# The last six chunks as three wide blocks, the weight sums on POOL, and two plain chunks ordered by a modelled clock

## The chip, the core and the metric

The kernel runs on one core of a Trainium2 chip: TensorE (PE, with its weight loads as PEld), VectorE (DVE), ScalarE (ACT), GpSimd (POOL) and SyncE (SP), whose queue issues nearly all transfers. The metric is the device time of the program in microseconds (us), a median over executions of one program.

## The reference

Windowed attention for 8 batches, 8 heads, 576 positions and 64 values a head, half of the heads with a dilation of 4, and behind it two matrix products with an ELU between them:

```python
attn = exp(scores - max) / (sum + 1e-9)          # window of 32, dilation 1 or 4
x = (attn @ v)  as  4608 tokens x 512
h = x @ w_in                                      # 512 x 2048
g = where(h > 0, h, exp(min(h, 0)) - 1)
out = g @ w_out                                   # 2048 x 512
```

## The kernel before, in words

**Precision.** A float32 product runs as three products of a faster format: each operand is split into a rounded part (a cast) and what is left (the "rest", the operand less its rounded part), and high x high, high x low and low x high are summed in PSUM. A cast is ACT's as a rule, a rest is DVE's.

**Tokens.** The 4608 tokens are nine chunks of 512. Chunks 0, 1 and 2 are *plain*: for each of 16 blocks `f` of 128 hidden units, 12 products make `h` in a PSUM bank, the ELU and the split are done, and 12 products add the block to four output banks `o_ps`. In chunk 0 the first blocks run in full float32, and the weights arrive and are converted there.

**Chunks 3 and 4 are *combined*** (`combined_chunk`): the first matrix product is done by a scheme of seven products in place of eight (Winograd's form of Strassen's), with sums of weight blocks (S1 to S4) and of token blocks (T1 to T4, made by `moving_operand`). A step has 12 products of 256 columns. The second matrix product stays plain: 16 blocks, 4 token tiles and 3 products each, 192 of 512 columns a chunk, taken from a list `fifo` between the steps.

**Chunks 5 to 8 are two *wide blocks*** (`wide_chunk`) of two chunks each. Both matrix products use the scheme there, `inner` for the first (28 units of 12 products of 512 columns) and `outer` for the second (28 units of 12). `make_unit` makes a unit's operand ahead of time, `summed` the token sums that it needs.

**Weights.** The sums of the weights' blocks are made on the chip and written to DRAM (`combined`, `sums_out`). The sums of the first weights are made in `combine`, on DVE with casts on ACT, in chunks 1 and 2; those of the second in `combine_out`, on POOL with casts on ACT, in chunks 3 to 5. `load_combined` brings each unit's weights, 512 KB, back into a ring `r0` of four, on SP's queue.

**Attention.** Batches 0 and 1 are done in chunk 0. A *piece* is either the scores of a pair of heads (36 small products of 64 columns) or its outputs (12 of 96 columns), put between other products. For batches 2 and 3, `scores_piece` and `outputs_piece` do two pairs at a time, in three banks (both `a_ps` and `h1`), at blocks named by `WHEN`; from chunk 3 on `pieces` does one pair at a time, in the two `a_ps` banks. Later batches' outputs go by DRAM (`outputs`) until their token chunk comes.

**What sets the order.** In chunks 0 to 2 a scheduler orders the instructions, held by `issue_after` where the program says so. From chunk 3 on the program order holds: `clock` models the time of PE, DVE, ACT and POOL, `side` holds lists of steps (softmax, weight sums), and `work(until)` issues those steps that the modelled clock can finish by a time. Each engine, and each queue, takes its instructions in order.

In a plain chunk after the first, ACT copies `h` out of its PSUM bank (`elu`, L874), and exp (L879), a relu (L888) and the max step (L889) read the copy. Chunks 1 and 2 use one bank `h0` for this, since `h1` is a pieces' bank. L149 is `mm`, which issues every product; L629 is `Ordered`, which issues all that the modelled clock orders; in the changed program these are L146 and L606.

Of the kernel before, what the change touches and what calls it, by code (L numbers as in the profile page):

```python
# [24 lines left out]
P = 128  # L25
# [8 lines left out]
LASTC = NCH - 4  # L34
# [16 lines left out]
ORDER = "A11 S2 S3 A12 S1 A22 S4".split()  # L51
STORED = "A11 A12 S2 S4 S3 S1 A22".split()
MOVING = "B11 T2 T3 B21 T1 T4 B22".split()
POPS = (3, 4, 0, 4, 0, 5, 0)
FIRST_POPS = (2, 2, 1, 2, 1, 1, 2), (3, 4, 3, 2, 0, 4, 0)
TODO = [t.split() for t in ("u1 exp0< relu0< rest1<", "u2 elu0< cast0<", "u3 rest0<", "C11", "C22", "C21 exp1 relu1 push1", "elu1 C12 cast1 push0")]
OPERANDS = [t.split() for t in ("", "cast:B11 make:T1", "rest:B11", "make:T2 cast:T2", "rest:T2", "make:T3", "cast:T3 rest:T3",
                                "cast:B21 rest:B21", "make:T4 cast:T1", "rest:T1 cast:T4", "rest:T4 cast:B22", "rest:B22", "", "")]
WHEN = {1: (0, 6, 7, 13), 2: (1, 6, 7, 12)}
LAST = 14  # L60
OPER = 12
PLAIN = ("a5", "a-1'", "a3'", "a4'", "r1'", "r2'")
HALVED = {(2, 3): 4}
COMBINE = {(1, 11): 0, (1, 13): 1, (1, 15): 2, (2, 2): 3, (2, 4): 4, (2, 6): 5, (2, 9): 6, (2, 11): 7}
PLAN = {36: "R5", 52: "X0", 55: "X2"}
WIDE_PLAN = {5: "R6"}
OUTPUTS_FROM = 7
KEPT_UNTIL = 18
PIECES_AT = range(7, 42)
COMBINE_AT = {2: "F0", 4: "C0", 6: "W0", 8: "F1", 10: "C1", 12: "W1", 14: "F2", 16: "C2", 18: "W2", 36: "F3", 39: "C3", 40: "W3", 41: "F4", 44: "C4", 45: "W4", 46: "F5", 49: "C5", 50: "W5"}  # L70
WIDE_COMBINE = {9: "F6", 13: "C6", 14: "W6", 15: "F7", 18: "C7", 19: "W7"}
FIRST = 6
# [3 lines left out]
KEEP = {0: (14, 15, 12, 13, 0, 1, 2, 3), 3: (4, 5), 4: (6, 7), 6: (8, 9), 8: (10, 11)}  # L76
# [8 lines left out]
WIDE_OPERANDS = {(2, 3): "cast:B11", (2, 4): "rest:B11", (3, 1): "cast:B21", (3, 2): "rest:B21"}  # L85
WIDE_FIRST = {"A11": "make:T1 make:T2 cast:T2 rest:T2", "A12": "cast:T1 rest:T1 make:T3", "S2": "cast:T3 rest:T3 make:T4", "S1": "cast:T4 rest:T4", "S3": "cast:B22 rest:B22"}
STORE_LAG = 1
STEP = 1.28
# [3 lines left out]
LANDING = 6.0  # L92
TOLERANCE = 0.3
SURE = -3.0
ENDING = 1.9
EASE = 0.4
OVERRUN = (1.5, 2.5, 1.5, 2.5, 2.5, 2.5, 1.0)
# [6 lines left out]
def body(ctx: ExitStack, tc: tile.TileContext, q, k, v, masks, w_in, w_out, out, out_t):  # L104
# [24 lines left out]

    raw2, raw, full4, full2, full = [None] * (NF // 2), [None] * NF, [None] * (NF // 2), [None] * NF, [None] * 2 * NF  # L130
# [15 lines left out]
    def mm(to, w, x, **kw):  # L146
        n = length(x)
        clock["PE"] += n * (4.0 if x.dtype == F32 else 1.0) / 2400 if n != 2 * G else 0.062
        return inorder(nc.tensor.matmul(to, w, x, **kw))  # L149
# [1527 lines left out]
```

## Time and profile before

| | |
|---|---|
| median of 3 runs | 849.73 us (849.23 to 850.75) |
| the profiled execution's own time | 847.88 us |
| its span, first to last instruction | 846.1 us |
| mean granted TensorE clock | 0.998 |
| busy: PE, DVE, ACT, POOL | 830.7, 642.2, 546.5, 76.7 us |
| read from and written to HBM | 148.0 and 49.5 MB |

A group's row reads: line, engine, operation, output <- inputs, shapes, count | busy us, mean ns of one | idle us of the engine just before, and what ended it. A row of a stage reads: from:to, length, busy us (count) of PE, PEld, DVE, ACT and POOL, granted clock, share of the DMA engines, GB/s. A float32 product of 64 or 96 columns has two records, so 12 products of 96 columns show as x24. Chunk 1 begins near 127 us, chunk 3 near 318, the first wide block at 515, the last at 690.

### The profile page before, as it was taken

The numbers are of one execution on the slowest core, as the hardware profiler recorded it, in microseconds if no ns is written. First come the engines' busy times: TensorE is split into PE (matmuls) and PEld (weight loads), VectorE is DVE, ScalarE is ACT, GpSimd is POOL, SyncE is SP. The second block draws the span as 40 slices with busy tenths as digits, with TensorE's granted clock in tenths as the row PEclk, the third lists the DMA queues.
The fourth block names the chain that finished last, engine by engine and source line by source line (L and its number), as shares of the span: only waits on it lengthen the run. The fifth ranks groups of instructions, "written<-read, shape, count | busy, mean of one in ns | idle before, by whom it ended". The sixth has DMA issues, their size and how long they took to land.

```text
span 846.1 us, 16853 instructions
## 1 busy us (share of the span) xinstructions
PE 830.7 (98%) x6696; PEld 676.1 (80%) x6696; DVE 642.2 (76%) x871; ACT 546.5 (65%) x935; POOL 76.7 (9%) x78
## 2 busy tenths in 40 slices
PE   6999999999999999999999999999999999999998
PEld 5566888888888887888888988878788888888886
DVE  6999998868588878788676777584879763466992
ACT  5888776645655556677667767667964535686450
POOL 3000000000000002330011330013202020000000
PEclk9999999999999999999999999999999999999999
DMA  9997466532687877998889995667756677666665
GB/s 308 371 380 298 133 186 222 170 114 100 205 252 250 244 205 254 317 322 259 242 262 336 322 324 186 236 187 253 255 182 202 194 245 216 193 196 196 195 212 169
DMA packets 105934, 198.67 MB, mean 235 GB/s; under 512 B 13216, under 2 KB 58112, under 8 KB 105600
## 3 DMA queue, kind: packets, MB, share of 16 engines
q1 hardware_dynamic: 105712, 197.29, 71.9%
q8 instruction: 53, 0.87, 0.4%
q10 hardware_dynamic: 144, 0.31, 0.1%
q14 instruction: 25, 0.20, 0.1%
HBM read 148.02 MB, written 49.55 MB: 233 GB/s over the span
## 4 chain that ended last, share of the span: by engine, by line
PE 95%; DMA 2%; DVE 1%; ACT 1%; SPq 1%; issue 0%; POOL 0%; DVEq 0%; ACTq 0%; POOLq 0%
PE o_ps L149 48%; PE h L149 35%; PE a_ps L149 11%; DMA outputs<-gl 1%; DMA r<-combined 1%; DMA qt<-q 0%; PE a L149 0%; ACT pt L538 0%; PE b L149 0%; SPq L319 0%; DVE nmx L498 0%; POOL r L463 0%; DVE pt L536 0%; PE d L149 0%; DVE sm L463 0%
## 5 line engine op out<-in xcount | busy, mean ns | idle before, releaser
L149 PE MATMUL o_ps<-a,r 128*128 128x512 f32 x672 | 159.6, 390 | 0.0
L149 PEld LDWEIGHTS o_ps<-a,r 128*128 128x128 f32 x672 | 125.1, 188 | 25.8
L149 PE MATMUL h<-x,r 128*128 128x256 f32 (+1 forms) x708 | 131.2, 335 | 0.4 <-issue 0.4
L149 PEld LDWEIGHTS h<-x,r 128*128 128x128 f32 x708 | 108.5, 189 | 16.6 <-ACT x L629 0.8
L149 PE MATMUL o_ps<-r,r 128*128 128x512 f32 x384 | 93.6, 389 | 0.0
L149 PE MATMUL h<-a,r 128*128 128x512 f32 (+1 forms) x456 | 89.3, 347 | 1.4 <-ACT e L629 1.3
L149 PEld LDWEIGHTS h<-a,r 128*128 128x128 f32 x456 | 73.5, 189 | 13.8 <-ACT e L629 1.8
L149 PEld LDWEIGHTS o_ps<-r,r 128*128 128x128 f32 x384 | 71.6, 188 | 14.6
L149 PE MATMUL o_ps<-a,gh 128*128 128x512 f32 x216 | 75.1, 445 | 0.0
L149 PEld LDWEIGHTS o_ps<-a,gh 128*128 128x128 f32 x216 | 40.2, 188 | 17.3 <-issue 10.5
L874 ACT COPY h<-h 128x512 f32<-128x512 f32 x30 | 17.5, 582 | 40.0 <-PE h L149 39.9
L149 PE MATMUL o_ps<-r,gh 128*128 128x512 f32 x128 | 40.2, 395 | 0.0
L149 PE MATMUL a_ps<-a,r 128*128 128x512 f32 x168 | 39.4, 389 | 0.0
L894 DVE TENSOR_TENSOR gl<-e,gh 128x512 fp32r<-128x512 f32 x37 | 25.4, 686 | 17.5 <-ACT gh L893 17.1
L149 PEld LDWEIGHTS a_ps<-a,r 128*128 128x128 f32 x168 | 31.5, 188 | 6.5
L629 ACT COPY pt<-sm 32x384 f32<-32x384 f32 x48 | 24.5, 510 | 17.2 <-DVE sm L629 16.5
L629 ACT ACTIVATE x<-x 128x1024 f32<-128x1024 f32 (+1 forms) x33 | 34.9, 1056 | 0.5
L149 PE MATMUL h<-x,a 128*128 128x512 f32 (+1 forms) x128 | 34.3, 416 | 0.0
L149 PEld LDWEIGHTS a_ps<-pt,vt 128*64 128x64 f32 x640 | 27.2, 137 | 8.4 <-issue 5.2
L629 POOL TENSOR_TENSOR h<-h 128x256 f32<-128x256 f32 x24 | 23.8, 993 | 109.6 <-DMA kt<-k 51.8
L149 PE MATMUL a_ps<-pt,vt 128*64 128x96 f32 x640 | 31.9, 250 | 0.1
L149 PE MATMUL o_ps<-a,gl 128*128 128x512 f32 x80 | 31.3, 391 | 0.0
(259 smaller groups left out, 1631.4 us busy)
## 6 DMA issues: line engine op xcount, KB each, us to landing
r<-combined SPq DMA_DIRECT2D x112, 512.0 KB, 4.6
r<-sums_out SPq DMA_DIRECT2D x32, 512.0 KB, 4.6
r<-plain_out SPq DMA_DIRECT2D x24, 512.0 KB, 4.3
vt<-v SPq DMA_DIRECT2D x30, 384.0 KB, 4.7
kt<-k SPq DMA_DIRECT2D x29, 304.0 KB, 4.4
qt<-q SPq DMA_DIRECT2D x30, 288.0 KB, 4.3
r<-w_in SPq DMA_DIRECT2D x16, 512.0 KB, 6.9
r<-w_out SPq DMA_DIRECT2D x16, 512.0 KB, 7.7
```

What stands on the lines that cost most here:

```text
L149: return inorder(nc.tensor.matmul(to, w, x, **kw))
L629: return inorder(getattr(self.eng, name)(**kw))
L874: copied.append(a.copy(out=h, in_=h_ps).ins)
L894: low.append(v.tensor_tensor(out=gl, in0=e, in1=gh.bitcast(F32), op=ALU.subtract).ins)
```

## The change

- Chunks 3 to 8 are three wide blocks. `combined_chunk`, its operands and its list of steps are gone; plain chunks remain for 0, 1 and 2.
- Chunks 1 and 2 (`plain_chunk`) are now in program order by the modelled clock too. A block's ELU and split are steps (`own_steps`) that go first; `late_steps` (splits of weights), softmax steps and weight sums follow as they fit. After each run of 12 products (`slot`) one piece, of one pair, may be put.
- exp and the max step read `h` in its PSUM bank; the copy is gone, and the banks `h0` and `h1` alternate.
- All 16 weight sums are jobs (`start_sums`) whose adds, casts and rests are on POOL, from block 7 of chunk 1 into the first wide block. Some softmax steps and splits of weights go to POOL or to their own engine, whichever the clock frees first (`better`). In the first wide block POOL makes the token sums of `summed`, and operands are made at most four units ahead.
- The outputs of batch 4 go by DRAM too, and the first weights of the wide blocks are loaded in block 14 of chunk 2.
- The modelled clock has new prices for products, for POOL and for what POOL adds to DVE.

Three places in the instruction lists show what moves. First TensorE, in the part that was the first combined chunk; `h_4246` and `h_4353` are its two banks, `o_ps` a bank of the second product. Before:

```order
L149 MATMUL h_4246<-r_1358,r_934 128x256 x12
L149 MATMUL h_4353<-x_3440,r_934 128x256 x12
L149 MATMUL o_ps<-a_1961,a_1626 128x512 x2
L149 MATMUL o_ps<-a_1961,a_1681 128x512
L149 MATMUL o_ps<-a_1961,a_1626 128x512 x2
L149 MATMUL o_ps<-a_1961,a_1681 128x512
```

Now, at the entry of the first wide block, with products of chunk 2 between its first units:

```order
L146 MATMUL a_ps_4072<-r_1352,r_932 128x512 x6
L146 MATMUL a_ps_4073<-r_1352,r_932 128x512 x6
L146 MATMUL o_ps<-r_1321,gh 128x512 x2
L146 MATMUL o_ps<-r_1321,gl 128x512
```

A unit's 12 products have 512 columns instead of 256, and there are half as many units for the same tokens.

Second, the sums of the first weights. Before, they stand on DVE in chunks 1 and 2, among the ELU's steps (`a_2284` holds a pair of weight blocks):

```order
L894 TENSOR_TENSOR gl<-e,gh 128x512
L302 TENSOR_TENSOR a_2284<-a_2284 128x256
L606 STREAM_TRANSPOSE pt_79<-sm 32x12x32 x6
L303 TENSOR_TENSOR a_2284<-a_2284 128x256
L889 SCALAR_TENSOR_TENSOR e<-h,e 128x512
L304 TENSOR_TENSOR a_2284<-a_2284 128x256
L305 TENSOR_TENSOR a_2284<-a_2284 128x256
L894 TENSOR_TENSOR gl<-e,gh 128x512
L309 TENSOR_TENSOR a_2284<-a_2284,e 128x512 x2
```

Now they stand on POOL, in the second half of chunk 1, with their casts and with softmax steps (`a_2073` holds the weights):

```order
L606 TENSOR_TENSOR sm<-sm,nmx 96x768
L606 TENSOR_TENSOR a_2073<-a_2073 128x256 x7
L606 COPY pt_79<-hh 32x12x32
L606 CAST e<-a_2073 128x512
L606 TENSOR_TENSOR a_2073<-a_2073 128x256
L606 CAST e<-a_2073 128x512
L606 TENSOR_TENSOR a_2073<-a_2073,e 128x512
L606 TENSOR_TENSOR sm<-sm,sums 96x768
L606 TENSOR_TENSOR a_2073<-a_2073,e 128x512
```

Adds, casts and rests of a sum follow each other on one engine, and DVE has none of them.

Third, the entry of the first wide block in the changed program. On DVE, from the last block's max step to the rest of T2 (`x_4088` is T1, `x_4089` T2, `a_1644` and `a_1745` T2's two parts, `a-1_3421` holds a softmax and the first columns of batch 4):

```order
L606 SCALAR_TENSOR_TENSOR e<-h_4022,e 128x512
L606 TENSOR_REDUCE sums<-a-1_3421 96x12
L606 TENSOR_TENSOR gl<-e,gh 128x512
L606 TENSOR_SCALAR sums<-sums 96x12
L606 RECIPROCAL sums<-sums 96x12
L606 TENSOR_TENSOR x_4088<-x_2761,x_1957 128x2x192
L606 TENSOR_TENSOR x_4088<-x_2761 128x2x64
L606 TENSOR_TENSOR x_4088<-a-1_3421,x_2761 128x2x256
L606 TENSOR_TENSOR x_4089<-x_2761,x_4088 128x2x192
L606 TENSOR_TENSOR x_4089<-x_2761,x_4088 128x2x64
L606 TENSOR_TENSOR x_4089<-a-1_3421,x_4088 128x2x256
L606 TENSOR_TENSOR a_1745<-x_4089,a_1644 128x2x512
```

And on SP's queue there (`r_932` is the ring of weights, `combined` the weight sums and blocks in DRAM):

```order
L315 DMA sums_out_113<-gh 128x2x256
L952 DMA r_932<-combined_89 128x1024
L315 DMA sums_out_113<-gh 128x2x256
L913 DMA out<-gh 128x512
L315 DMA sums_out_113<-a_2073 128x2x256
L913 DMA out<-gh 128x512
L913 DMA out<-gl 128x512
L952 DMA r_932<-combined_88 128x1024
L315 DMA sums_out_113<-a_2073 128x2x256
L952 DMA r_932<-combined_88 128x1024
L340 DMA x_4088<-whole_out_106 128x1024
```

Before, T1 to T4 were made in chunk 2, and stores of POOL's sums stood between weight loads in the combined chunks.

The diff, cut to its core:

```diff
-LASTC = NCH - 4
+LASTC = NCH - 6
...
+FILL = 4.2
+EARLY = 0.0
+HOME = {2: 1, 3: 2, 4: 2.4, 5: 3.2, 6: 3.2, 7: 4.2}
+LEAD = 4
+SLOWING = 0.1
...
-        clock["PE"] += n * (4.0 if x.dtype == F32 else 1.0) / 2400 if n != 2 * G else 0.062
+        clock["PE"] += PIECES.get(n) or n * (4.0 if x.dtype == F32 else 1.0) / 2400 + 0.0133
...
-    def combine(p):
...
-        nc.vector.tensor_tensor(out=a22, in0=a21, in1=a22, op=ALU.add)
...
-            nc.scalar.copy(out=h, in_=w)
-            nc.vector.tensor_tensor(out=l, in0=w, in1=h.bitcast(F32), op=ALU.subtract)
...
+    def start_sums():
+
+        for half in (0, 1) if phase[0] < 3.4 else (2,):
+            if not jobs or busy[half] == "running" or (busy[half] or 0.0) > clock["PE"]:
+                continue
+            start_sum(half)
+
+    def start_sum(half):
...
+        nc.sync.dma_start(out=w, in_=(whole if kind == "in" else whole_out)[p])
...
+            steps.append([("sums", kind, p, len(steps)), pool, "tensor_tensor", dict(out=to, in0=x, in1=y, op=op)])
...
+            steps.append([("sums", kind, p, len(steps)), pool, "tensor_copy", cast, DM])
...
+            steps.append([("sums", kind, p, len(steps)), pool, "tensor_tensor", rest, DM])
...
+                if self.name == "POOL":
+                    clock["DVE"] += SLOWING * self.cost(kw)
...
+    def better(step, since):
+
+        name, eng, op, kw, *more = step
+        if name[0] not in SHARED or not phase[0] < SHARED_UNTIL:
+            return step
+        other = [name, pool, {"copy": "tensor_copy"}.get(op, op), kw, *more]
+        return min(step, other, key=lambda x: max(x[1].free(), since) + cost(x))
...
+    def own_steps(c, f, h_ps):
+
+        e, g = [], live.setdefault((c, f), [])
+
+        def exp():
+            e.append(fp.tile([P, TC], F32, name="e"))
+            return dict(out=e[0], in_=h_ps, func=AF.Exp)
...
+        return [[("exp!", c, f), act, "activation", exp, TC],
+                [("relu!", c, f), act, "activation", lambda: dict(out=e[0], in_=e[0], func=AF.Relu, scale=-1.0, bias=1.0), TC],
+                [("stt!", c, f), vec, "scalar_tensor_tensor", lambda: dict(out=e[0], in0=h_ps, scalar=0.0, in1=e[0], op0=ALU.max, op1=ALU.subtract), TC],
+                [("cast!", c, f), act, "copy", split(lambda: dict(out=g[0], in_=e[0])), TC, high.append],
+                [("rest!", c, f), vec, "tensor_tensor", split(lambda: dict(out=g[1], in0=e[0], in1=g[0].bitcast(F32), op=ALU.subtract)), TC, low.append]]
...
-        h_ps = ps_h.tile([P, TC], F32, name=f"h{0 if 0 < c < B - 1 else f % 2}")
+        h_ps = ps_h.tile([P, TC], F32, name=f"h{f % 2}")
...
-            for s in (slice(0, HT), slice(HT, TC)) if t >= HALVED.get((c, f), TC) else (slice(0, TC),):
-                mm(h_ps[:, s], w[:, n * P:(n + 1) * P], x[:, s], start=t == 0, stop=t == len(terms) - 1 and s.stop == TC)
+            mm(h_ps, w[:, n * P:(n + 1) * P], x, start=t == 0, stop=t == len(terms) - 1)
...
-    stream = [("in", g, n) for _ in range(CS, LASTC) for g in range(NG) for n in ORDER] + wide * NW
+    stream = wide * NW
...
-    def combined_chunk(c):
...
-                    vec.tensor_tensor(out=to, in0=x, in1=y, op=ALU.subtract)
+                    (pool if w == 0 else vec).tensor_tensor(out=to, in0=x, in1=y, op=ALU.subtract)
...
-                if k < (inner_done[0] if k < len(ring) else outer_done[0] + len(ring)):
+                if k < min(inner_done[0] if k < len(ring) else outer_done[0] + len(ring), outer_done[0] + (LEAD if w == 0 else len(ring))):
...
+    def slot(c, f):
+
+        if (c, f) >= (1, 2) and not (c == 2 and f == NF - 1):
+            pieces()
+        if (c, f) >= (1, SUMS_FROM):
+            start_sums()
+        if c == 2:
+            firsts(CS + 1)
+        tick()
+
+    def plain_chunk(c):
+
         for f in range(NF):
+            late_until[0] = LATE_AT[min(f, len(LATE_AT) - 1)] if c == 1 else 12
+            phase[0] = c + f / 20
+            if c == 1:
+                while late_next[0] < late_until[0]:
+                    side.append(late_steps(late_next[0]))
+                    kept_lists.append(side[-1])
+                    late_next[0] += 1
+                if 0 < f < 6:
+                    until("late", f)
+            if f > 1 or c == 2:
+                until("stt!", *((c, f - 2) if f > 1 else (c - 1, NF - 2 + f)))
+            gemm = gemm1(c, f)
+            clock["now"] = clock["PE"]
+            if (c, f) == (1, NF - 1):
+                split_x(2, vec, act)
+            side.append(own_steps(c, f, gemm))
+            kept_lists.append(side[-1])
+            finished[id(side[-1])] = clock["PE"] + LATENCY
+            if c == CS - 1 and f in (13, 14):
+                name = ("B11", "B21")[f - 13]
+                wide_operand(0, "cast:" + name)
+                wide_operand(0, "rest:" + name)
+            pend.append((c, f, None))
+            slot(c, f)
+            work(clock["PE"] + FILL)
...
+                load_combined(RING)
+            flush(1 if (c, f) == (1, NF - 1) else LAG)
+            clock["now"] = clock["PE"]
+            slot(c, f)
+            work(clock["PE"] + FILL)
...
-    for c in range(CS, LASTC):
-        combined_chunk(c)
+        until("rest!", c, f)
+        fifo.extend((c, f, t, *live[c, f]) for t in range(TC // P))
```

More of the change, by code (lines that the diff above doesn't have):

```diff
@@ L643, in emit_next, with cost @@
         at[name] = clock[eng.name]
+        if more and callable(more[-1]):
+            more[-1](ins.ins)
+    def cost(step):
+        return step[1].cost(step[4] if callable(step[3]) else step[3])
+    CLASSES = "exp! relu! stt! cast! rest! late".split()
+    def better(step, since):
[4 more added lines that the diff above has]
+        return min(step, other, key=lambda x: max(x[1].free(), since) + cost(x))
     def work(until):
@@ L650, in work @@
             for n, pair in enumerate(side):
-                if ready_for(pair[0][0]):
-                    _, eng, _, kw = pair[0]
-                    start = max(eng.free(), finished.get(id(pair), 0.0))
-                    if start + eng.cost(kw) <= until:
-                        starts.append((start, pair[0][0][0] == "sums", n))
+                key = pair[0][0]
+                if ready_for(key):
+                    step = better(pair[0], finished.get(id(pair), 0.0))
+                    start = max(step[1].free(), finished.get(id(pair), 0.0), floor(key))
+                    if start + cost(step) <= until:
+                        starts.append((start, 0 if key[0][-1] == "!" else 1 if key[0][:4] == "late" else 3 if key[0] == "sums" else 2, n))
             if not starts:
@@ L666, in ready_for, with floor @@
     def ready_for(key):
+        if key[0] == "sums" and key[3] == 4 and casting[0] not in (None, key[1:3]):
+            return False
+        if key[0] == "rest!" and key[2] > 1:
+            return (key[1], key[2] - 2) in second_done
+        if key[0][:4] == "late":
+            return key[1] < late_until[0]
         return key[0] != "placed" or before_it(*key[1:3]) in taken_out
+    def floor(key):
+        return second_done.get((key[1], key[2] - 2), 0.0) + LATENCY if key[0] == "rest!" else 0.0
     def until(*key):
@@ L1156, in wide_chunk, with unused @@
     def wide_chunk(w):
-        base = (LASTC - CS) * NG * 7 + w * len(wide)
+        base = w * len(wide)
         blocks, banks_of = {}, {}
+        def unused(sm):
+            assert all(sm not in (kw.get("in_"), kw.get("in0")) for pair in side for *_, kw in (x[:4] for x in pair) if not callable(kw))
         def two(where):
@@ L1606, in body @@
+    split_x(1, vec, act, lambda: copies(*last_outputs, act))
+    pend.append((0, NF - 2, next(ends[0])))
+    split_w(NF - 1, 0, 2, None, vec, act)
+    next(ends[1])
+    next(ends[1])
+    pend.append((0, NF - 1, next(ends[1])))
+    for j in KEEP[0]:
+        keep_whole(j)
+    sms.append([ap.tile([QB, 2 * NU, 2 * G], F32, name="sm", bufs=1), None])
+    hh.append(fp.tile([P, 2, TC], F32, name="hh", bufs=1))
+    other_sm(hh[-1])
     clock["now"] = clock["PE"]
-    clock["DVE"] = clock["PE"] + ENDING
@@ L1608, in body @@
-    finished.update((id(pair), clock["PE"] + ENDING) for pair in side)
+    clock["DVE"] = clock["ACT"] = clock["PE"] + START
+    for c in (1, 2):
+        plain_chunk(c)
     for c, f, g in pend:
-        fifo.extend((c, f, t, *g) for t in range(TC // P))
-    pop(2)
-    for c in range(CS, LASTC):
-        combined_chunk(c)
+        until("rest!", c, f)
+        fifo.extend((c, f, t, *live[c, f]) for t in range(TC // P))
     for w in range(NW):
```

682 lines of the change are left out of this document (237 added, 445 removed).

## The prediction

> **What bounds the kernel now.** I read the page's busy times and chain first, then the busy time of each engine by stage, then the time one product takes, from the chain.
>
> ```profile
> PE 830.7 (98%) x6696; PEld 676.1 (80%) x6696; DVE 642.2 (76%) x871; ACT 546.5 (65%) x935; POOL 76.7 (9%) x78
> PE 95%; DMA 2%; DVE 1%; ACT 1%; SPq 1%; issue 0%; POOL 0%; DVEq 0%; ACTq 0%; POOLq 0%
> ...
> 117.00:313.00 196.00, 195.96 (x1687) 159.99 (x1691) 156.81 (x280) 114.47 (x213) 0.47 (x5) 1.00 0.64 200
> 313.00:515.00 202.00, 199.51 (x2253) 173.39 (x2239) 153.58 (x205) 146.12 (x236) 42.26 (x36) 1.00 0.88 288
> 515.00:690.00 175.00, 174.94 (x979) 142.91 (x978) 128.95 (x142) 112.40 (x151) 24.11 (x19) 1.00 0.67 212
> ```
>
> The last three rows are, to a few us, the end of chunk 0 with chunks 1 and 2, the two combined chunks, and the first wide block with its attention pieces. Their columns are PE, PEld, DVE, ACT and POOL, each as busy us. TensorE leaves 0.04, 2.49 and 0.06 us idle in them, so 573 us of the program run at the pace of TensorE's stream. A change is then worth what it takes out of that stream, less what it makes the stream wait. "Busy" alone would not prove a full pace, since products overlap in the records; the time from one product's start to the next does:
>
> ```profile
> 374.33 2.87 PE h L149 x24
> 820.46 21.77 PE o_ps L149 x96
> ```
>
> In rows of the chain (start, us), 24 products of 256 columns in a combined chunk take 2.87 us, 0.1196 each. In a wide block, 96 of 512 columns take 21.77 us, 0.2268 each. Two narrow ones cost 0.239, so 5% more than one wide product of the same columns.
>
> **The products.** The lists of the two programs give the counts. The change removes 672 narrow products of the combined chunks and 16 narrow ones of chunk 2 (a halved product), 688 x 0.1196 = 82.3 us. It removes 384 wide ones (the second matrix product of two chunks, 16 blocks x 4 x 3 each) and adds 672 for the third wide block (336 for its first product, 336 for its second) and 8 in place of the halved 16: 296 more, x 0.2268 = 67.1 us. Together **-15.2 us**. About 11 us of it are the 48 products that seven eighths of the second matrix product save, and the rest is the narrow products' overhead.
>
> **The attention pieces.** Their arithmetic stays, but pairs that were done two at a time in chunks 1 and 2 are now single, and each break in the stream costs.
>
> ```profile
> 119.79 2.88 PE L149 MATMUL h<-x,r 128*128 128x512 f32 x12
> 122.60 1.21 PE L149 MATMUL a_ps<-pt,vt 128*64 128x96 f32 x24
> 123.74 0.74 PE L149 MATMUL o_ps<-r,gh 128*128 128x512 f32 x2
> ...
> 124.56 0.63 PE L149 MATMUL o_ps<-r,gh 128*128 128x512 f32 x2
> ...
> 126.64 2.88 PE L149 MATMUL h<-x,r 128*128 128x512 f32 x12
> ...
> 130.35 0.74 PE L149 MATMUL o_ps<-r,gh 128*128 128x512 f32 x2
> ...
> 166.78 0.39 PE L149 MATMUL o_ps<-a,gl 128*128 128x512 f32 x1
> 167.10 1.87 PE L149 MATMUL a_ps<-pt,vt 128*64 128x96 f32 x40
> 168.80 0.50 PE L149 MATMUL h<-pt,vt 128*64 128x96 f32 x8
> 169.23 3.01 PE L149 MATMUL h<-x,a-1_857 128*128 128x512 f32 x12
> ```
>
> Twelve wide products end at 119.79 + 2.72 = 122.51; the next product starts at 123.74. A single pair's outputs cost 1.23, and the first rows behind take 0.74 instead of 0.63, so 1.34 in all. Two pairs together cost 169.23 - 166.78 - 0.23 + 0.11 = 2.33. The new list has 8 more singles and 4 fewer doubles: 10.7 - 9.3 = +1.4. A run of 36 scores costs 130.35 - 129.36 + 0.11 = 1.10; there are two more of these, for one run of 72 gone (1.8 by the same rows): +0.4. Together **+1.8 us**, and the stream changes by -13.4.
>
> **The ELU reads its bank.** Thirty copies go from ScalarE, and exp and the max step read PSUM themselves. The bank is then held until the max step has read it.
>
> ```profile
> L874 ACT COPY h<-h 128x512 f32<-128x512 f32 x30 | 17.5, 582 | 40.0 <-PE h L149 39.9
> L879 ACT ACTIVATE e<-h 128x512 f32<-128x512 f32 x44 | 27.3, 621 | 0.5 <-PE h L149 0.3
> L888 ACT ACTIVATE e<-e 128x512 f32<-128x512 f32 x30 | 19.0, 633 | 0.8
> L889 DVE SCALAR_TENSOR_TENSOR e<-h,e 128x512 f32<-128x512 f32 x30 | 20.5, 686 | 5.3 <-ACT e L888 5.2
> ...
> L629 DVE TENSOR_TENSOR sm<-a_ps,masks_sb 96x384 f32<-96x384 f32 x16 | 8.1, 542 | 2.6 <-PE a_ps L149 2.6
> ```
>
> 0.62 + 0.63 + 0.69 is 1.9 us, 2.7 at most with the hand-overs. The two banks now alternate, so the next product into the same bank starts three runs of 12, 8.2 us, later. I cost the hold at nothing; that gap hides it, and with a single bank (2.7 us) it would not. The 17.5 us of ACT copies were not on TensorE's path either (ACT idles 40 us before them), so they bring nothing. The three-bank score pieces and their memset go as well; two banks taken by a single pair are read by two mask adds, 2 x 0.54 us, within the 2.7 us of the next run.
>
> **All weight sums on POOL.** This is the edit that can cost. POOL gains 32 adds of 256 columns (0.99), 18 of 512 (1.56), 17 of 1024 and a dozen smaller operand pieces (2.6 and about 1.3), 32 casts and 16 attention steps (about 1.3). DVE loses the sums of the first weights, 48 short transposes for 8 long ones, and operands of half width. Counted over the lists with the durations of such rows, it has 35 us less work of its own.
>
> ```profile
> L629 POOL TENSOR_TENSOR h<-h 128x256 f32<-128x256 f32 x24 | 23.8, 993 | 109.6 <-DMA kt<-k 51.8 <-DMA h<-whole_out 29.7 <-DVE sums L629 13.9
> L629 POOL TENSOR_TENSOR h<-h,gh 128x512 fp32r<-128x512 f32 x12 | 18.4, 1555 | 36.5 <-ACT gh L629 36.3
> L629 POOL TENSOR_TENSOR x<-x,x 128x896 f32<-128x896 f32 x3 | 7.7, 2579 | 45.0 <-issue 45.0
> ...
> L606 DVE STREAM_TRANSPOSE pt<-sm 32x384 f32<-32x384 f32 x48 | 27.3, 568 | 0.7
> L629 DVE STREAM_TRANSPOSE pt<-pt 128x1152 f32<-128x1152 f32 x16 | 21.9, 1372 | 2.5 <-ACT pt L629 2.5
> L305 DVE TENSOR_TENSOR a<-a 128x256 f32<-128x256 f32 x8 | 3.4, 422 | 0.2
> L629 DVE TENSOR_TENSOR sm<-sm,sums 96x768 f32<-96x768 f32 x8 | 8.7, 1093 | 0.0
> L463 DVE TENSOR_TENSOR sm<-sm,sums 96x768 f32<-96x768 f32 x13 | 12.4, 952 | 0.2
> L629 DVE TENSOR_TENSOR r<-a,r 128x1024 fp32r<-128x1024 f32 x10 | 14.2, 1416 | 9.3 <-ACT r L629 9.3
> L629 DVE TENSOR_TENSOR a<-r,a 128x1024 fp32r<-128x1024 f32 x20 | 24.3, 1218 | 4.2 <-ACT a L629 4.2
> ...
> 593.57 3.18 DVE L629 TENSOR_TENSOR r<-a,r 128x1024 fp32r<-128x1024 f32 x1 [4.85 <-ACT r L629]
> ...
> 593.55 2.12 POOL L629 TENSOR_TENSOR x<-x,x 128x896 f32<-128x896 f32 x1
> ```
>
> No POOL cast of a float stands in the trace; between nothing and an add of the same width (1.56) I take 1.3, since one operand is read instead of two. POOL's new work is then about 180 us, most of it in chunks 1, 2 and the first wide block, some 365 us in which DVE, at 77% as now, idles about 85 (439 busy of 573 in the stages above). POOL itself is far from full. But DVE pays: the same step takes 1093 ns where POOL works and 952 in the chunks where it does not; another group 1416 against 1218. Such differences, over all groups of 768 and 1024 columns in the table by form, come to about 9 us for the 66 us that POOL is busy from 313 to 690, 0.14 us of DVE per us of POOL. The dearest single case in the last two rows is 1.96 us over 3.18, 0.62. So the cost to DVE is 25 us at the mean, 0 at the low end and 112 at the high end. I take the mean, since many POOL operations stand behind it. DVE then stays near 77% and hides it: -35 + 25.
>
> The Trainium skill (SBUF — State Buffer, "SBUF: two separate sides") speaks against this edit: the port pair that GpSimd and VectorE share is an exclusive lock, and the later one "fully blocks" for the whole instruction. The row at 593.57 agrees (2.0 us waited behind a 2.12 us POOL add); the group means show that most steps do not meet it. By the page alone, with every POOL us lost to DVE, DVE would need 180 us more against 85 idle and the sum would be an estimated 931; the same mechanism, priced from rows, is the slower rival (c).
>
> **The order, and waits that go or come.** The combined chunks had these waits:
>
> ```profile
> 321.95 1.69 PE L149 MATMUL h<-a,r 128*128 128x256 f32 x12 [1.33 <-ACT e L629]
> ...
> 317.75 0.47 SPq L319
> ...
> 319.43 0.68 SPq L337
> ...
> 320.20 4.57 DMA r<-combined
> ...
> L629 ACT CAST a<-r 128x1024 fp32r<-128x1024 f32 x20 | 21.0, 1051 | 15.7 <-DVE r L629 11.9 <-PE a_ps L149 3.0 <-PE h L149 0.8
> ...
> r<-combined SPq DMA_DIRECT2D x112, 512.0 KB, 4.6
> ```
>
> The chain shows that the first is a late weight load, 4.57 us behind a row of stores on SP's queue. The new list loads the first four weights during the last fills of chunk 2, so this goes, with the rest of the 2.49 us. New at the entry of the first wide block: operand T2 is made on DVE right behind the last ELU. Its chain from the first unit's start is the max step, a row sum, the rest, two operands of 1024 columns in three pieces each (about 1.5), a cast of 1.05 and a rest of 1.22: some 8 to 9 us. The third unit needs it 48 products, 10.9 us, later; 0 to 2 us may be lost if DVE comes late. Queued behind T2 on DVE are the first block sums. I set the new waits equal to the old ones, 2.5 us.
>
> **Sum.** 847.88 - 15.2 + 1.8 = 834.5 for an execution like the profiled one. The shown median is 1.85 above that execution, so **836 us**; 833 to 839 is this case's own range.
>
> **Rivals.**
> (a) *No new wait*, 833: chunks 1 and 2 ran with 0.04 us idle, the later wide block too. Against it: a longer list of POOL and SP work is new there.
> (b) *Late weights in the first wide block.* SP's queue now holds stores of POOL's sums and of chunk 2's outputs between the weight loads. Such a store waits for its producer, with the next load behind it. The ring is three units ahead, 8.2 us, against 4.6 to land: 3.6 us of slack, while one pair of POOL's casts and rests takes 5.7. Three loads late by 2 to 3 us each give 842 to 845. For it: the wait at 321.95 is of this kind.
> (c) *POOL drags DVE until DVE sets the pace: slower.* At 0.62 us per POOL us DVE gets 112 us more where it has 85 idle; 27 us come to the path, 863. It is slower than before from (85 + 13) / 180 = 0.54. For it: the row at 593.57; against it: the mean of 0.14.
> (d) *The order doesn't do what it says*, the clock misjudging DVE, so that fills wait for their rest: 1 us for every third of 32 fills gives 847.
>
> **Chances.** Forecast 0.55, (a) 0.15, (b) 0.15, (d) 0.05, (c) 0.10. Changes under 0.2% (1.7 us) can't be told from none. Faster is the first three and 0.03 of (d), 0.88; within 0.2% the rest of (d) and 0.01 of (c), 0.03; slower 0.09. The range, 831 to 846, leaves out (c) and the outermost of (a).
>
> **What would show it.** 688 fewer narrow products at 0.2268 a wide one, and a third block of 152 us like the last one; PE idle under 3 us from 117 to the second block; DVE's 1024-column steps at 1.3 to 1.5 us beside POOL. It is wrong if those steps go near 2 us and PE waits for DVE or for r<-combined by more than 10 us in all.

## The result, and the profile after

The changed kernel takes 859.42 us in the median (858.76 to 860.48) against 849.54 us of the kernel before beside it: a ratio of 1.0115, with a 95% interval of 1.0097 to 1.0132. It is 1.2% slower; the forecast was 836 us, 831 to 846. The profiled execution has a span of 858.6 us, 12.5 more than before.

The page of the changed kernel, busy times first, then the chain, then the granted clock in 40 slices:

```profile
PE 827.7 (96%) x6304; PEld 653.9 (76%) x6304; DVE 649.5 (76%) x769; ACT 539.9 (63%) x912; POOL 230.9 (27%) x200
...
PE 83%; DVE 8%; ACT 5%; DMA 2%; issue 2%; DVEq 0%; SPq 0%; ACTq 0%
...
PEclk9999999999999999999999879999999999999999
```

TensorE has fallen from 95% of the chain to 83%; DVE holds 8% of it. DVE's share of the span is 76%, as before. The clock dips in slices 23 and 24, where it did not before. The stages (PE, PEld, DVE, ACT and POOL busy, granted clock, DMA) and the waits of TensorE from 117 us on say where:

```profile
117.00:341.00 224.00, 219.68 (x2267) 174.58 (x2266) 172.24 (x239) 140.75 (x259) 100.98 (x103) 1.00 0.68 210
341.00:475.00 134.00, 128.92 (x1034) 102.35 (x1033) 108.89 (x116) 97.36 (x147) 66.79 (x51) 0.99 0.84 276
475.00:520.00 45.00, 35.32 (x195) 26.98 (x194) 38.48 (x32) 21.48 (x29) 36.55 (x16) 0.85 0.53 166
520.00:700.00 180.00, 179.97 (x999) 147.33 (x998) 126.78 (x138) 105.67 (x140) 14.05 (x11) 1.00 0.68 209
```

```profile
PE o_ps L146 <- DVE a L606: 3.3, 1, 3.3
PE a_ps L146 <- issue: 3.1, 2, 2.1
PE o_ps L146 <- DVE r L606: 2.5, 1, 2.5
PE a_ps L146 <- DVE pt L606: 2.4, 1, 2.4
PE o_ps L146 <- ACT r L606: 2.4, 1, 2.4
...
PE h L146 <- ACT r L606: 1.1, 1, 1.1
...
PE o_ps L146 <- DMA r<-sums_out: 0.3, 1, 0.3
```

The last block of chunk 2 begins its `h` at 336 us, the wide blocks follow from 341, and the first of them ends at 541.9. TensorE idles 4.3, 5.1 and 9.7 us in the first three stages and nothing behind them. In the 45 us in which the first block's second matrix product begins, POOL is busy for 36.6. All 13 rows of waits (7 shown) add up to 19.0 us, against 2.4 before, in the same window of that kernel's trace:

```profile
PE h L149 <- ACT e L629: 1.7, 2, 1.3
PE h L149 <- issue: 0.4, 1, 0.4
PE a_ps L149 <- ACT gl L629: 0.3, 1, 0.3
```

What ended last around 490 us, from the chain (start, us):

```profile
483.12 2.84 DVE x L606
...
487.56 1.05 ACT r L606
...
488.64 2.91 DVE r L606
...
492.48 2.38 DVE r L606
...
500.51 3.07 DVE a L606
...
503.62 5.06 PE o_ps L146 x11
```

DVE rests (`r`, `a`) that take 1.22 us elsewhere take 2.4 to 3.1 here, the product of a softmax (`x`) 2.84, and TensorE waits behind them. The last row holds a second loss: 11 products in 5.06 us, 0.46 each, twice the 0.2268 of a full clock. Windows on either side show the granted clock:

```profile
489.00:496.00 7.00, 4.55 (x11) 3.48 (x11) 6.96 (x6) 2.20 (x4) 7.00 (x3) 0.52 0.03 12
496.00:503.00 7.00, 3.71 (x15) 2.46 (x13) 6.93 (x6) 2.73 (x3) 7.00 (x4) 0.99 0.49 150
503.00:510.00 7.00, 6.38 (x16) 5.04 (x17) 4.92 (x4) 4.09 (x7) 7.00 (x5) 0.52 0.10 9
```

I added up, over all products of both traces, the time from one start to the next beyond the pace of that kind of product. Above 250 ns it is a wait; some 0.2 us more per wide product is half a clock; the rest are the small breaks at the attention's pieces.

```
                before   after   difference
waits            13.6    32.8     +19.2
half clock       13.6    19.0      +5.4
small breaks     14.5    17.9      +3.4
products (forecast)               -15.2
sum                               +12.8   (spans: +12.5)
```

So the 15.2 us were saved, and 28 us came on top: 19.2 of waits, 5.4 of half clock, and 3.4 of small breaks, in which the forecast 1.8 of the attention pieces are contained.

### The profile page after: what moved, and what is told of

Read it like the earlier page. It is cut to its first block, busy times and chain, and to the rows that moved or that the text cites. A ratio compares the mean times of both kernels' runs of the same rounds, so it can differ in the third digit from the quotient of the medians.

```text
span 858.6 us, 16052 instructions
## 1 busy us (share of the span) xinstructions
PE 827.7 (96%) x6304; PEld 653.9 (76%) x6304; DVE 649.5 (76%) x769; ACT 539.9 (63%) x912; POOL 230.9 (27%) x200
## 4 chain that ended last, share of the span: by engine, by line
PE 83%; DVE 8%; ACT 5%; DMA 2%; issue 2%; DVEq 0%; SPq 0%; ACTq 0%
PE o_ps L146 43%; PE h L146 26%; PE a_ps L146 13%; DVE a L606 2%; DVE x L606 2%; DMA outputs<-a-1_3421 2%; ACT x L606 2%; DVE r L606 1%; ACT pt L533 1%; PE b L146 1%; ACT a L606 1%; DVE a-1_3421 L606 0%; DMA qt<-q 0%; DVE sm L606 0%; DVE pt L606 0%
## 5 line engine op out<-in xcount | busy, mean ns | idle before, releaser
L146 PE MATMUL o_ps<-a,r 128*128 128x512 f32 x792 | 191.6, 397 | 4.3 <-DVE a L606 3.3
L146 PEld LDWEIGHTS o_ps<-a,r 128*128 128x128 f32 x792 | 150.6, 191 | 37.6 <-DVE a L606 3.6
L146 PE MATMUL h<-a,r 128*128 128x512 f32 x396 | 94.7, 391 | 1.1 <-ACT r L606 1.1
L146 PE MATMUL h<-x,r 128*128 128x512 f32 x324 | 80.3, 395 | 0.0
L146 PEld LDWEIGHTS h<-x,r 128*128 128x128 f32 x324 | 59.9, 188 | 14.6 <-DVE x L606 1.1
L606 ACT ACTIVATE x<-x 128x1024 f32<-128x1024 f32 (+1 forms) x52 | 54.3, 1046 | 13.4 <-DVE x L606 12.7
L146 PE MATMUL a_ps<-a,r 128*128 128x512 f32 x252 | 60.4, 393 | 1.2 <-DVE a L606 1.2
L606 POOL TENSOR_TENSOR a<-a 128x256 f32<-128x256 f32 (+1 forms) x57 | 52.5, 924 | 31.9 <-DMA a<-whole_out 20.3
L606 DVE TENSOR_TENSOR a<-r,a 128x1024 fp32r<-128x1024 f32 x30 | 42.3, 1411 | 8.7 <-ACT a L606 8.6
L606 ACT CAST a<-r 128x1024 fp32r<-128x1024 f32 x30 | 31.5, 1050 | 14.5 <-DVE r L606 12.3
```

The source lines that it names most:

```text
L606: return inorder(getattr(self.eng, name)(**kw))
```

## The experiments

Waits by stage, in us, by the same reckoning (above 250 ns; "half" is half clock behind 117 us), for the runs below. Stages shift by a few us between runs. The kernel before, timed beside each group of runs, had medians of 849.0 to 849.8 us, so differences of about a microsecond between groups mean nothing.

```
run                          222-341  341-420  420-475  475-520  520-700  half   median
after                          5.2      3.3      2.8     11.8      0.0     5.8   859.4
e1_sums_dve                    6.3      2.3      2.4      6.0      0.0     1.4   850.9
e2_lead7                       5.0      3.8      3.3     14.9      0.0     2.2   863.6
e3_sums_dve_lead7              4.3      3.7      2.6      6.1      0.0     2.2   852.6
f1_shared_home                 5.7      2.3      3.9      5.8      0.0     3.6   851.5
f2_no_weight_adds              4.4      2.9      2.7      5.8      0.6     1.4   849.9
g6_margins                     2.5      3.5      4.8     11.5      0.0     4.6   856.6
k1_less_softmax                4.1      2.3      0.0      5.9      0.0     1.0   846.4
h1_outer6                      3.8      4.2      1.6      3.3      0.0     1.2   847.1
n6_home_outer6                 5.2      2.5      3.3      4.3      0.5     1.0   847.5
q6_early15                     4.5      2.0      1.8      2.1      1.1     1.6   846.0
q4_early05                     3.3      1.7      2.7      1.5      1.0     0.0   842.7
r1_no_weight_adds              7.6      1.3      2.9      2.9      0.0     4.2   851.5
s1_order_only                  6.6      1.8      2.3      4.8      2.6     2.8   851.9
p4_order_sums                  6.3      1.6      2.7      1.5      1.0     2.0   847.3
```

### The block sums on POOL

In the changed kernel the 16 sums of blocks behind the first block's ELU (`summed`) run on POOL, and `LEAD` lets its outer units be made at most four ahead. In the diff below `as_pool` issues on DVE and moves the planner's clock as POOL does. Theory A: the sums starve the units. Theory B: POOL slows DVE everywhere.

```diff
 e1_sums_dve
+    as_pool = Ordered(nc.vector, "POOL", 0.55, 0.0017)
-                    (pool if w == 0 else vec).tensor_tensor(out=to, in0=x, in1=y, op=ALU.subtract)
+                    (as_pool if w == 0 else vec).tensor_tensor(out=to, in0=x, in1=y, op=ALU.subtract)
```

> The changed kernel, with the 16 block sums of the first wide block's second product computed on DVE instead of POOL; the planner still prices them as POOL work, so the order of all other instructions stays. Theory A (these sums on POOL starve the outer units between 475 and 520 us): the waits over 250 ns there, 11.8 us, and the 4.4 us lost at half clock behind them fall below 2 us together, and the time to 843-848. Theory B (POOL's work slows DVE everywhere, and no one place decides): DVE takes 16 x 1.22 = 20 us more, POOL's 45 us go and with them some 0.3 x 45 = 13 us of drag, so the units come as late as now: 856-862.

Measured: 850.86 us, 8.6 less than the changed kernel; against before 1.0029 (1.0011 to 1.0048). Half of the waits from 475 to 520 went, with most of the half clock. A in direction; its "below 2" was wrong, 6 us stayed, and the time lies between the two theories' ranges.

```diff
 e2_lead7
-LEAD = 4
+LEAD = 7
```

> The changed kernel, with the outer units of the first wide block made up to 7 ahead, as in the kernel before, instead of 4; the sums stay on POOL. Theory A1 (four units ahead are too few for the chain POOL sum, ACT cast, DVE rest): three units more are 3 x 5.4 = 16 us of cover, the waits from 475 to 520 go: 843-848. Theory A2 (POOL is full there, 36.6 busy of 45 us, so the sums can't be had earlier): POOL has room before (20 of 55 us busy from 420 to 475), so about half goes: 849-854. Theory B: no change, 857-861.

Measured: 863.62 us, 1.0167 (1.0146 to 1.0187): four slower than with four units ahead. No theory had that. Earlier units put more rests that wait for a POOL sum into DVE's queue ahead of the attention's steps: one wait of 7.2 us at 484 is for DVE's mask add of a score. The lead of four eases what the sums cost.

The same edits in the kernel before, where nothing else changes:

```diff
 b1_before_pool_sums
-                    vec.tensor_tensor(out=to, in0=x, in1=y, op=ALU.subtract)
+                    (pool if w == 0 else vec).tensor_tensor(out=to, in0=x, in1=y, op=ALU.subtract)
```

> The kernel before, with one part of the change alone: the 16 block sums of its first wide block on POOL instead of DVE (units still up to 7 ahead). Theory A: POOL has 16 x 2.9 = 46 us more in a stage where it was busy for 24 of 175; if the sums by themselves starve the units, +8 to +16: 858-866; if it takes the lead of four as well, within 2 us of before: 848-852. Theory B: DVE loses 20 us of own work and gets 0.3 x 46 = 14 us of drag: no change, 848-851.

Measured: 858.07 us, 1.0107 (1.0082 to 1.0133), +9. The sums alone cost nearly as much as the whole change did: TensorE, by the reckoning of the table, waits 7.5 us in the first wide block, where it did not wait before. That is Theory A's number, not B's. This run shows why. DVE and POOL groups from 620 to 660 us, of this run and then of the kernel before:

```profile
L629 DVE TENSOR_TENSOR a<-r,a 128x1024 fp32r<-128x1024 f32 x4 | 11.2, 2843 | 0.0
L629 DVE TENSOR_TENSOR gh<-o_ps,h 128x512 f32<-128x512 f32 x2 | 1.3, 676 | 0.0
...
L629 POOL TENSOR_TENSOR r<-r 128x1024 f32<-128x1024 f32 x4 | 13.3, 3352 | 0.0
```

```profile
L629 DVE TENSOR_TENSOR a<-r,a 128x1024 fp32r<-128x1024 f32 x4 | 4.9, 1217 | 0.0
L629 DVE TENSOR_TENSOR gh<-o_ps,h 128x512 f32<-128x512 f32 x2 | 1.3, 685 | 0.0
```

A rest goes from 1217 to 2843 ns, while the step that reads PSUM stays at 0.68 us. Single rows of this run (start, us) show them take turns:

```profile
637.89 3.41 DVE L629 TENSOR_TENSOR a<-a,a 128x1024 fp32r<-128x1024 f32 x1
640.18 3.37 POOL L629 TENSOR_TENSOR a-1_3444<-a,a-1_3444 128x1024 f32<-128x1024 f32 x1
641.23 6.75 DVE L629 TENSOR_TENSOR r<-r,r 128x1024 fp32r<-128x1024 f32 x2
643.52 3.38 POOL L629 TENSOR_TENSOR a<-a,a 128x1024 f32<-128x1024 f32 x1
```

Each takes 3.4 us, in lockstep. The shortest POOL sum of this kind in the changed kernel is 2.34 us (at 488.13); 2.34 and 1.22 are 3.56. The pair takes nearly as long as the two one after the other: while DVE has such steps to run, a sum moved to POOL costs it more than the 1.22 us that it took there. The Trainium skill (SBUF — State Buffer, "SBUF: two separate sides") calls the shared port pair an exclusive lock; for these steps the trace agrees.

```diff
 b2_before_pool_sums_lead4 (beside the edit of b1)
-                if k < (inner_done[0] if k < len(ring) else outer_done[0] + len(ring)):
+                if k < min(inner_done[0] if k < len(ring) else outer_done[0] + len(ring), outer_done[0] + (4 if w == 0 else len(ring))):
```

> The kernel before, with the 16 block sums of its first wide block on POOL and the units there at most 4 ahead. Theory A1 (lead and POOL together): the waits of the changed kernel appear, +10 to +16: 860-866. Theory B: 848-852, as with the sums alone.

Measured: 854.17 us, 1.0063 (1.0038 to 1.0087), +5. A1 falls here too: the shorter lead takes four us off.

### What the other 17 us are

With the sums on DVE the kernel is still 15 us above the forecast. The next four runs start from both edits (e1 and e2).

> The changed kernel with both edits: block sums of the first wide block on DVE, and its units up to 7 ahead. Theory C (with the sums on DVE, the lead of four is what is left too short: 6.0 us of waits and 1.4 at half clock from 475 to 520 in the run with the sums alone): these go, 843 to 846. Theory D (DVE, busy 42 of 45 us there, sets the pace): they stay, 849 to 852.

Measured: 852.63 us, 1.0041 (1.0027 to 1.0055). Theory C falls: waits from 475 to 520 stay at 6.1.

In chunks 1 and 2 the planner may give a step of `SHARED` to POOL (`better`); the next edit keeps it on its own engine at POOL's price:

```diff
 f1_shared_home
-        other = [name, pool, {"copy": "tensor_copy"}.get(op, op), kw, *more]
+        other = [name, Ordered(eng.eng, "POOL", 0.55, 0.0017), op, kw, *more]
```

> As the run with both edits, and the attention's and the late weights' steps that the planner gives to POOL in chunks 1 and 2 run on DVE and ACT, still priced as POOL's, so that the order stays. Theory B (contention: of the waits from 222 to 420 us, 8.6 us, a good part is DVE slowed by POOL): a third of POOL's steps there are gone, 1 to 3 us faster than the run with both edits. Theory E (those waits are the order's: pieces of attention stand in TensorE's list before their operand can be there): DVE has some 10 us more to do, 0 to 3 us slower.

Measured: 851.53 us, 1.0013 (0.9998 to 1.0028). One us less than e3, hardly more than the two intervals can tell apart.

The steps left out in the next run are issued by an engine object that moves the planner's clock and emits nothing:

```diff
 f2_no_weight_adds
-            steps.append([("sums", kind, p, len(steps)), pool, "tensor_tensor", dict(out=to, in0=x, in1=y, op=op)])
+            steps.append([("sums", kind, p, len(steps)), no_pool, "tensor_tensor", dict(out=to, in0=x, in1=y, op=op)])
...
-            steps.append([("sums", kind, p, len(steps)), pool, "tensor_tensor", rest, DM])
+            steps.append([("sums", kind, p, len(steps)), pool if n else no_pool, "tensor_tensor", rest, DM])
```

> As the run with both edits, but 64 adds of 256 columns and 16 rests of 512 of the weight sums are left out on POOL (the sums are then wrong; the loads, casts, last rests and stores stay, and the planner prices the steps as before): some 85 us of POOL's work gone. Theory B (contention): the waits from 222 to 420 us fall from 8.6 to below 3, 5 to 8 us faster than the run with both edits. Theory E (order): they stay above 6, within 2.5 us of it.

Measured: 849.89 us, 1.0003 (0.9989 to 1.0018), 2.7 less than e3. From 222 to 341 us (PE, PEld, DVE, ACT, POOL), e3 and then f2:

```profile
222.00:341.00 119.00, 115.62 (x1249) 90.97 (x1237) 91.05 (x123) 72.22 (x135) 62.86 (x68) 1.00 0.68 215
```

```profile
222.00:341.00 119.00, 115.33 (x1252) 91.32 (x1251) 84.74 (x122) 71.84 (x135) 24.55 (x29) 1.00 0.68 214
```

POOL has 38 us less to do and DVE gets 6 us back, but TensorE is as idle as before. The weight sums on POOL do slow DVE; in this stage that is not what TensorE waits for. Theory B falls for it. The profiled executions of the two runs differ by only 0.6 us, so the traces don't show where the 2.7 us of the medians come from.

```diff
 g6_margins
-SLOWING = 0.1
+SLOWING = 0.2
-EARLY = 0.0
+EARLY = -1.0
-PIECES_AT = range(7, 44)
+PIECES_AT = range(7, 48)
```

> As the run with both edits, but the planner's clock charges DVE 0.2 us instead of 0.1 for each us that POOL works, and puts a piece of attention into TensorE's list of chunks 1 and 2 only 1 us after it expects the operand, not at once; pieces may stand in four more units of the first wide block. Theory E (order): the waits from 222 to 420 us fall by 4 or more, 3 to 6 us faster than the run with both edits. Theory B (contention alone): the same drag, pieces later in place of waits; within 2 us of it.

Measured: 856.57 us, 1.0074 (1.0046 to 1.0101). The waits from 222 to 341 fell from 4.3 to 2.5, but the pieces that come later met the outer units: one wait of 11.2 us at 491, for a bank whose reader stood late in ACT's queue. Later pieces move the waits to a dearer place.

One thing about `EARLY` that the expectations of this run and of q6 have wrong: the kernel uses it only up to the first block of chunk 2, and `TOLERANCE` from there on (chunk and block number make up `phase[0]`):

```python
... <= clock["PE"] + (TOLERANCE if phase[0] > 2 else EARLY)
```

In the changed kernel chunk 2 begins at 231 us. The waits counted from 222 to 341 us are nearly all chunk 2's, so an edit of `EARLY` reaches them only through what it shifts in chunk 1. Neither g6 nor q6 tests directly whether chunk 2's pieces stand too early.

The next runs start from e1.

```diff
 k1_less_softmax (in e1)
-        yield ("max", b, hp), vec, "tensor_reduce", dict(out=mx, in_=sm, op=ALU.max, axis=mybir.AxisListType.X)
+        yield ("max", b, hp), no_dve if b in (5, 6) else vec, "tensor_reduce", dict(out=mx, in_=sm, op=ALU.max, axis=mybir.AxisListType.X)
```

("less" and "times" in the same way.)

> The changed kernel with the block sums on DVE (lead of four), and three of DVE's softmax steps (max, less, times; 0.94 + 0.95 + 0.95 us) left out for the eight pairs of batches 5 and 6, which are done in the first wide block; their outputs are then wrong, the planner prices the steps as before and the order stays. 23 us of DVE's work are gone, next to none of POOL's. Theory D (with the sums off POOL, DVE's own load in the first wide block sets the waits: it is busy 42 of the 45 us from 475 to 520): the 8.4 us of waits and 1.4 at half clock from 420 to 520 fall below 3, 842 to 846. Theory E (the hand-overs of the order): they stay above 6, 848 to 851.

Measured: 846.40 us, 0.9956 (0.9941 to 0.9972). The waits from 420 to 475 went, those from 475 to 520 stayed at 5.9. From 420 to 520 that is 8.4 us down to 5.9: neither below 3, as D had it, nor above 6, as E had it, and the time is 0.4 above D's range. DVE's load counts for a part; at the outer units something else does.

```diff
 h1_outer6 (in e1)
-OUTER_STEP = 12.0
+OUTER_STEP = 6.0
```

> The changed kernel with the block sums on DVE, and in the outer units of the first wide block the planner issues softmax steps only up to 6 us ahead of TensorE's clock instead of 12, so that fewer of them stand in DVE's queue ahead of the units' rests. Theory E (order): 3 to 6 us faster than with the sums alone on DVE, 845 to 848. Theory D (load): the same work, waits move but stay, 849 to 852.

Measured: 847.06 us, 0.9981 (0.9962 to 1.0000), with all of the softmax still there. Fewer softmax steps stand in DVE's queue ahead of the units' rests, and the waits from 475 to 520 fall from 6.0 to 3.3. Theory E, and the look-ahead alone: 3.8 us less than e1.

> As the last run, and the attention's and late weights' steps of chunks 1 and 2 on DVE and ACT instead of POOL, priced as POOL's. Theory B (contention in the chunks): 1 to 3 us faster than the last run. Theory D: DVE has some 10 us more to do in stages where it is 76% busy: within 2 us of the last run.

Measured: 847.53 us, 0.9972 (0.9960 to 0.9985): the edit of f1 on top of h1, no difference.

What such a hand-over looks like, in the changed kernel (start, us, engine, and in brackets the idle time and what ended it):

```profile
416.31 4.20 POOL L606 TENSOR_TENSOR x<-x,gh 128x512 fp32r<-128x512 f32 x2
...
417.34 2.03 DVE L606 TENSOR_TENSOR x<-x,nmx 96x768 f32<-96x768 f32 x1
419.41 0.84 ACT L606 ACTIVATE x<-x 96x768 f32<-96x768 f32 x1 [2.90 <-DVE x L606]
420.16 1.05 ACT L606 COPY r<-h 128x512 f32<-128x512 f32 x2
...
420.78 3.02 PE L146 MATMUL h<-a,r 128*128 128x512 f32 x12 [1.05 <-ACT r L606]
```

POOL's rests double a DVE step (2.03 in place of 0.95); ACT has that step's exponential at the head of its queue and waits 2.9 us; behind it stands the copy that frees TensorE's bank. The delay comes from POOL, the price from what is queued behind.

### Which of the two, and a version that is faster than both

Both start from n6.

```diff
 q6_early15
-EARLY = 0.0
+EARLY = -1.5
```

> As the run with the sums on DVE, the steps at home and 6 us of look-ahead, and a piece of attention goes into TensorE's list of chunks 1 and 2 only 1.5 us after the planner expects its operand. Theory E (the waits from 222 to 341 us, 5.2 us there, are hand-overs that the planner puts too early): they fall below 2 us, and if the pieces that come later cost nothing in the first wide block, 843 to 845; if they do (as in the run with margins), 847 to 850. Theory B (contention): the waits stay above 4.

Measured: 846.02 us, 0.9940 (0.9919 to 0.9962). The waits from 222 to 341 fell only from 5.2 to 4.5; the stage from 475 on gained 2. Theory E's "below 2" failed and the time lies in neither of its ranges; 4.5 is above B's 4. With `EARLY` acting in chunk 1 alone, this decides between the two for chunk 2 only in part.

```diff
 q4_early05
-OUTER_STEP = 6.0
+OUTER_STEP = 4.0
-EARLY = 0.0
+EARLY = -0.5
```

> As before, with 0.5 us in place of 1.5 and a look-ahead of 4 us in place of 6. Theory E: the waits from 222 to 341 us fall to 3 or 4, those from 420 to 520 stay near 7 or fall; 845 to 848.

Measured: **842.70 us, 0.9908 (0.9880 to 0.9936)**, 0.9% faster than the kernel before and 16.7 us faster than the changed one. The waits fell as E had it (3.3 us from 222 to 341, 4.2 from 420 to 520); the time is 2.3 below its range. The edit has two numbers, and how much each of them gives is not separated. Its stages:

```profile
117.00:341.00 224.00, 221.26 (x2277) 176.44 (x2276) 178.31 (x249) 146.75 (x271) 90.99 (x92) 1.00 0.70 217
341.00:475.00 134.00, 130.73 (x1116) 103.83 (x1115) 109.16 (x130) 98.04 (x147) 42.47 (x39) 1.00 0.86 283
475.00:520.00 45.00, 43.76 (x190) 35.09 (x189) 44.79 (x48) 27.32 (x38) 7.24 (x3) 1.00 0.66 198
```

From 475 to 520 DVE is busy for 44.8 of 45 us, more than in the changed kernel (38.5), and TensorE idles 1.2 us instead of 9.7. So a full DVE is not by itself what makes TensorE wait there: what counts is which step DVE does when, and whether POOL holds it up (POOL is busy for 7.2 us here, 36.6 in the changed kernel).

```diff
 r1_no_weight_adds (in n6)
 the two steps of f2, left out in the same way
```

> The run with the sums on DVE, the steps at home and 6 us of look-ahead, with 64 adds and 16 rests of the weight sums left out on POOL (the sums are wrong; the order stays): what POOL's remaining work in chunks 1 and 2 and the first wide block costs. Theory B: the waits from 222 to 520 us, 15 us, halve: 839 to 842. Theory E: 2 to 3 us less, 844 to 846.

Measured: 851.45 us, 1.0011 (0.9990 to 1.0032), slower than n6 with less work on POOL. The waits from 222 to 341 rose to 7.6. The weight adds' contention is not the missing 11 us (B and E both had gains here). A list that is timed for one pace of DVE may also lose when DVE is faster; that is a guess, and no run here shows it.

Last, the order alone on the changed kernel, and the sums on top of it:

```diff
 s1_order_only (in the changed kernel)
-OUTER_STEP = 12.0
+OUTER_STEP = 4.0
-EARLY = 0.0
+EARLY = -0.5
```

> The changed kernel with its block sums and softmax steps on POOL as they are, and only the two numbers of the order from the fastest run: 4 us of look-ahead in the outer units, attention pieces 0.5 us later. Theory F (order and block sums on POOL are two separate costs, 8 us each): 849 to 853. Theory G (once the softmax stands behind the units' operands, POOL's sums are covered): 842 to 846.

Measured: 851.93 us, 1.0024 (1.0006 to 1.0042). Theory F: the two numbers of the order give 7.5 us back. The waits from 475 to 520 fall from 11.8 to 4.8 us. Not all of it is order: the planner also chooses POOL for five steps fewer.

> The same order with the block sums on DVE and the softmax steps still on POOL. Theory F: the block sums' part comes off, 842 to 845, and the softmax steps on POOL are worth within 2 us of the fastest run. Theory B (contention in the chunks): 3 us or more slower than the fastest run.

Measured: 847.33 us, 0.9966 (0.9948 to 0.9983). This is s1 with the edit of e1: the sums' part is 4.6 us here. It is also q4 with the softmax and late weights' steps on POOL: 4.6 us slower than q4, as B had it, and against F, whose 842 to 845 it missed. Between the two only the engine of 14 steps differs, from POOL to DVE or ACT. In n6 the same edit brought nothing.

## Why the prediction was wrong, point by point

**The products: right.** In the last two blocks TensorE runs at the forecast pace (chain of the changed kernel, start and us):

```profile
520.14 21.76 PE o_ps L146 x96
...
833.10 21.77 PE o_ps L146 x96
```

96 products in 21.77 us are 0.2268 each, and the account above closes to 0.3 us with the -15.2.

**The attention pieces: nothing against them.** +1.8 was forecast; all small breaks together grew by 3.4, and the pieces' part is not separated.

**The ELU reads its bank: nothing seen against it.** Among TensorE's waits no bank of chunks 1 and 2 waits for the max step; the one row for `h` (1.1 us) is the wide block's copy at 420. It was not undone by itself.

**All weight sums on POOL: the step that failed.** It said "DVE then stays near 77% and hides it". DVE did stay at 76%, and hid nothing, on three counts.
- The size. POOL gained 154 us (180 forecast). Over DVE's steps that touch a POOL operation, the time beyond the median of the same shape alone is 51 us after and 10 before: 41 for 154, 0.27 us per POOL us in place of 0.14. A mean over all of POOL's work was the wrong price for 1024-column sums beside rests: in b1 these cost (2843 - 1217) / 3352, which is 0.49 us of DVE per us of POOL, nearer to the forecast's dearest row, 0.62.
- The place. I used DVE's idle share over 573 us as cover. What counts is the stage from 475 to 520: 16 sums in series, each in front of a cast and a rest, beside the last softmaxes. I listed the 16 among "17 of 1024" and never gave them a place. They cost 8.6 us, or 4.6 once the order is better.
- The softmax steps and splits of weights on POOL, up to 4.6 us (q4 against p4).

**The order and its waits: failed.** I "set the new waits equal to the old ones, 2.5 us", having priced T2 alone. T2 did wait (the waits on `a` at 357 and 364 us, 1.2 by the page), as the text allowed. But with two chunks fewer the attention's last pairs come in the outer units of the first block, whose operands stand in DVE's queue behind up to 12 us of softmax issued ahead: 7.5 us, by s1, which also puts chunk 1's pieces 0.5 us later. The look-ahead alone, at 6 us, gave 3.8 (h1 against e1).

**The rivals.** (a) no; (b) no: TensorE waited 0.3 us for a weight load. (c) named the right mechanism and side with the wrong place of decision: it asked for 98 us of drag to fill DVE, while 41 us, spent in front of a waiting TensorE, were enough; its chance of 0.10 was too low by that. By its own rule, slower only from 0.54 us of DVE per us of POOL, the measured 0.27 would have been no loss. (d) happened too, and larger: the 847 priced late fills, and the waits came at operands and attention pieces.

**The signs.** The "third block of 152 us" (702.5 to 854.9) and the pace held. "PE idle under 3 us" did not: it was 19. The sign of failure came in both its halves: 2148 ns for 1024-column steps inside POOL's operations, and 11.1 us of TensorE's waits for DVE among the 19.0.

**What stays open.** Of the 23.4 us above the forecast the runs account for 16.7: 7.5 for the order (s1), then 4.6 for the block sums (p4), then 4.6 for the other steps on POOL (q4). q4 is still 6.7 us above the forecast and has some 6 us more waits than before. The waits from 222 to 341 us changed between 2.5 and 7.6 us from run to run with edits that did not aim at them; no single cause of them is shown.

## What to carry to other kernels

Idle time of an engine over a long stage is no cover for work that stands in front of a waiting engine: find the stage in which the moved steps are in series with a consumer, and price them there. Steps with two inputs in SBUF that move from DVE to POOL are not relief when DVE runs steps of the same kind at that time; price each pair at the sum of both. Where an order is written out ahead, look at what waits behind the first step that comes late, and change the look-ahead before the engines.

## What the runs showed of the hardware

DVE's steps beside POOL fall into two kinds. Mean ns in the changed kernel, alone and inside a POOL operation for over nine tenths of their time (count of the latter):

```
tensor_tensor, two SBUF inputs, 128x1024     1218   2148  (14)
tensor_tensor, two SBUF inputs, 96x768        950   1570  (16)
tensor_scalar, 96x12                          163    804   (9)
tensor_tensor, one input in PSUM, 96x384      545    543  (16)
reduce, 96x768                                940    940  (19)
transpose, 128x1152                          1368   1366   (9)
scalar_tensor_tensor, 128x1024               1218   1338   (4)
```

So a softmax's max, sum and transposes go on beside POOL, and its subtraction and product do not. The last row, also a step with two SBUF inputs, looks like an exception and is not one. Its four cases began when a POOL step had 0.15 to 0.5 us left, and each ended 1.07 to 1.08 us after that step. Where POOL's step has just begun, the wait is long, as in h1:

```profile
423.51 1.57 POOL L606 TENSOR_TENSOR x<-x,x 128x640 f32<-128x640 f32 x1 [5.12 <-DMA sums_out<-x]
423.65 2.51 DVE L606 SCALAR_TENSOR_TENSOR r<-r,x 128x1024 f32<-128x1024 f32 x1 [0.98 <-ACT x L606]
```

How much such a step loses depends on what is left of the POOL step in front of it; the rows of the table differ by that too.

The clock: TensorE waited 2.5 and 2.7 us at 485.9 and 488.7, with one product between, and ran at half clock for 6.8 us from 489.3; the wait of 3.6 us at 499.8 was followed by 6.8 us of it from 502.9. The Trainium skill (TensorE: Matmul & The Clock Gate, "HAM oscillation — how this bites in real kernels") gives idle gaps over about 3.4 us as the cause. The wait at 499.8 agrees; the others are shorter. A single wait of 2.5 us at 440.9, with narrow products of 96 columns behind it, was also followed by 3.4 us at half clock, and one of 2.1 at 228.5 in q6 as well; a wait of 2.3 us at 253 was not, nor one of 2.65 at 696.6 in b2. So waits below 3.4 us can cost the clock here, and what decides which of them do is open. With the waits gone (q4) all of the 5.8 us came back.
